# The last matrix product of a decode step in two column groups of 256 columns instead of four of 128

## The chip, the core and the metric

The kernel runs on one core of a Trainium2 chip. The metric is the device time of one execution in microseconds, the median of several runs. The core has four engines that matter here: TensorE (PE; its weight loads are listed as PEld), VectorE (DVE), ScalarE (ACT) and GpSimd (POOL). SyncE (SP) issues the transfers. TensorE writes to PSUM, and VectorE and ScalarE copy from PSUM into SBUF.

## What is computed

One decode step of a transformer block for 8 sequences, one token each, model width 512: attention over the last 2048 positions of a cache (32 query heads, 8 key/value heads), then an MLP with 1792 hidden units. Each sits behind a LayerNorm and is added to its input. The token shift in the middle of the second block moves everything out of a sequence of length one, so that its product with `w2` is zero.

```python
def _A_ref(x, k_cache, v_cache, wq, wo):
    q = heads(x @ wq)
    k, v = last 2048 positions, each kv head for 4 query heads
    p = _softmax(q k^T * Dh ** -0.5)
    return (p @ v) @ wo

def _B_ref(x, w1, w2, w3, w4):
    ...                                   # hs is zero for S == 1
    x1 = x + hs
    h2 = _gelu(_layernorm(x1, axis=-1) @ w3) @ w4
    return x1 + h2

x = A_x
h = x + _A_ref(_layernorm(x, axis=-1), A_k_cache, A_v_cache, A_wq, A_wo)
h2 = h + _B_ref(_layernorm(h, axis=-1), B_w1, B_w2, B_w3, B_w4)
return h2
```

The change concerns the last line: `... @ w4`, the addition of `x1` and `h`, and the way of the sum into the output.

## The kernel before

The order of the work on each engine is written out by hand: the program appends operations to one list for each engine, each with the semaphores that it waits for, and emits the lists at the end. [...]

The bulk of the time is the stream of keys and values (16 tiles each of 2 MB), transposed and multiplied as they land. All big loads are issued by SP in a fixed order: keys, values, the parts of `wo`, then `w3` (L672) and, last of all, `w4` in three parts (L676). The parts cover rows 0 to 7, 8 to 11 and 12 to 13 of 14 blocks of 128 hidden units (`W4_AT = (0, 8, 12, FC)`, L634).

The tail after the last value tile goes: output projection (L490, L511, L520), LayerNorm statistics (L569 to L601), the product with `w3` (L588, 56 products of eight columns), Gelu (L613), and the last product with `w4`. The names that matter for the last product:

- `gT` holds the Gelu's result, hidden unit by row, 8 sequences and 24 zeros as 32 columns for each of the 14 blocks. It is the stationary operand, so a product has 32 output rows.
- `z_ps` is a part of one PSUM bank (`S_ps[1]`). Output column block `nb` (128 of the 512 columns) is put into rows 32 `nb` to 32 `nb` + 31, columns 0 to 127: the four blocks use the four column groups of TensorE (`tile_position=(0, 32 * nb)`).
- `pe_w4` (L640) runs over the blocks of one part of `w4`, and for each over the four column blocks, with `w4_sb` as the moving operand of 128 columns. It is called three times, and each call waits for its own part of `w4`; the first also for both halves of `gT` and for the bank.
- `pe_fin` (L630) adds the residual: `fin`, in a high and a low bf16 part (`fr[:, 0]` and `fr[:, 1]`, written at L621 and L622), is multiplied with the identity into the same accumulation. Its eight products stand between the first and the second part of `w4`.
- L647 to L652: four copies of 8 rows by 128 columns from `z_ps` to `out_sb`, alternately by VectorE and ScalarE, each waiting for the last product.
- L693: SP stores `out_sb` when the last copy of either engine is done. Nothing else is left then.

Of the kernel before, what the change touches and what calls it, by code (L numbers as in the profile page):

```python
# [7 lines left out]
ACT = mybir.ActivationFunctionType  # L8
# [3 lines left out]
B = 8  # L12
D = 512
H = 32
DH = 128
# [7 lines left out]
FC = F // 128  # L23
FG = FC // 2
KC = D // 128
# [49 lines left out]
def bass_sequential_preLN__sliding_block_cached__mixer_s_mlp__decode_kernel(  # L75
# [23 lines left out]
    with es:  # L99
# [7 lines left out]
        ident_b = sb([128, 128], dt.bfloat16, "ident_b")  # L107
# [10 lines left out]
        w4_sb = sb([128, FC, D], dt.bfloat16, "w4_sb")  # L118
# [53 lines left out]
        fr = qflat[:, 0:2 * KC * 32].rearrange("p (a n x) -> p a n x", a=2, n=KC)  # L172
        gT = qflat[:, 2 * KC * 32:(2 * KC + FC) * 32].rearrange("p (f x) -> p f x", f=FC)
        out_sb = orow[0:B, 0, :]
# [4 lines left out]
        S_ps = [ps_t([128, 512], dt.float32, f"S_ps{i}") for i in range(2)]  # L179
# [13 lines left out]
        PE, AC, DV, PO, SP = (Engine(S(n)) for n in ("s_pe", "s_act", "s_dve", "s_pool", "s_sp"))  # L193
# [21 lines left out]
        e = DV.op(lambda e: e.bn_stats(st6[:, :], x_sb[:, :]), X)  # L215
        e = DV.op(lambda e: e.bn_aggr(mv[:, :], st6[:, :]), e)
        e = PO.op(lambda e: e.tensor_scalar(rstd[:, :], mv[:, 1:2], EPS, None, ALU.add), e)
        e = PO.op(lambda e: e.tensor_tensor(rstd[:, :], rstd[:, :], half[0:B, 0:1], ALU.pow), e)
# [8 lines left out]
        e = DV.op(lambda e: e.tensor_reduce(hsq[:, :], ident_f[:, :].rearrange("p (u h) -> p h u", u=4), AX.X, ALU.add))  # L227
# [31 lines left out]
        e = PE.op(pe_xT, e_xln, e_idb)  # L259
# [6 lines left out]
        for j in range(2):  # L266
# [9 lines left out]
            if j == 0:  # L276
                e = AC.op(lambda e: e.activation(qrow[:, 0, :], S_ps[0][:, :], ACT.Copy, scale=inv_sqrt_dh), e_q)  # L277
            else:
                e = DV.op(lambda e: e.tensor_scalar(qrow[:, 1, :], S_ps[1][:, :], inv_sqrt_dh, None, ALU.mult), e_q)  # L279
# [285 lines left out]
        def bc(a):  # L565
            return bass.AP(tensor=a.tensor, offset=a.offset, ap=[a.ap[0], [0, KC], [1, B]])


        e = DV.op(lambda e: e.tensor_reduce(hsum[:, :], vr(hT_ps[:, 0:NH]), AX.X, ALU.add), e_wo[-1])  # L569
# [30 lines left out]
        e = AC.op(lambda e: e.activation(s2[:, :], vsum[:, :], ACT.Sqrt, bias=eps2[:, :], scale=1.0), e_vs)  # L600
        e_r2 = DV.op(lambda e: e.reciprocal(r2[:, :], s2[:, :]), e)  # L601

        def bcf(t):
            a = t[:, :]
            return bass.AP(tensor=a.tensor, offset=a.offset, ap=[a.ap[0], [0, FH], [1, B]])
# [3 lines left out]
        for n in range(2):  # L609
            cs = slice(n * FH * B, (n + 1) * FH * B)  # L610
            e = DV.op(lambda e, n=n, cs=cs: e.tensor_tensor(v3(g_x[:, cs]), v3(y_ps[n][:, 0:FH * B]), bcf(r2),
                                                            ALU.mult), e_y[n], e_r2)
# [3 lines left out]
        e = PO.op(lambda e: e.tensor_scalar(r1[:, :], vsum[:, :], EPS * (1.0 + EPS), None, ALU.add), e_vs)  # L616
        e = PO.op(lambda e: e.tensor_tensor(r1[:, :], r1[:, :], half[:, :], ALU.pow), e)
        e = DV.op(lambda e: e.tensor_tensor(v3(xb[:, :]), v3(hc[:, :]), bc(r1[:, :]), ALU.mult), e)
# [2 lines left out]
        e_fr = DV.op(lambda e: e.tensor_copy(fr[:, 0, :, 0:B], v3(fin[:, :])), e_fin, e_gz)  # L621
        e_fr = DV.op(lambda e: e.tensor_tensor(fr[:, 1, :, 0:B], v3(fin[:, :]), fr[:, 0, :, 0:B], ALU.subtract), e_fr)  # L622

        z_ps = S_ps[1][:, 0:DH]

        def pe_fin():
            def f(e):
                for part in range(2):
                    for nb in range(KC):
                        ins = e.matmul(z_ps[32 * nb:32 * (nb + 1), :], fr[:, part, nb, :], ident_b[:, :],  # L630
                                       start=False, stop=False, tile_position=(0, 32 * nb), skip_group_check=True)
                return ins
            PE.op(f, e_fr)
        W4_AT = (0, 8, 12, FC)  # L634
        for n, waits in enumerate(((*e_gT, free[1]), (), ())):
            lo, hi = W4_AT[n:n + 2]
            def pe_w4(e, lo=lo, hi=hi):
                for fc in range(lo, hi):
                    for nb in range(KC):
                        ins = e.matmul(z_ps[32 * nb:32 * (nb + 1), :], gT[:, fc, :],  # L640
                                       w4_sb[:, fc, nb * 128:(nb + 1) * 128], start=(fc == 0), stop=(fc == FC - 1),
                                       tile_position=(0, 32 * nb), skip_group_check=True)
                return ins
            if n == 1:
                pe_fin()
            e_z = PE.op(pe_w4, (sem_w4[n], 16), *waits)
        for nb in range(KC):  # L647
            to, got = out_sb[:, nb * 128:(nb + 1) * 128], z_ps[32 * nb:32 * nb + B, :]
            if nb % 2:
                e_outa = AC.op(lambda e, to=to, got=got: e.activation(to, got, ACT.Copy), e_z)  # L650
            else:
                e_outd = DV.op(lambda e, to=to, got=got: e.tensor_copy(to, got), e_z)  # L652

        def load_k(j):
            dma(SP, knat[:, j % NK, :],
# [72 lines left out]
```

## Time and profile before

| | us |
|---|---|
| runs, median (lowest to highest of 3) | 194.07 (194.07 to 194.26) |
| the profiled execution | 193.93 |
| its span | 192.6 |
| PE busy in the span | 153.9 |
| DVE busy | 99.6 |
| ACT busy | 95.2 |
| last w4 product's end to the copies' start (L640 to L652) | 190.50 to 190.56 |
| the store's issue (L691) | 191.25 to 191.63 |

The span is the part of an execution between the first and the last recorded instruction; 1.3 us lie around it. For most of it the transfers are the limit: the 16 DMA engines move some 430 GB/s in nearly each slice, and in the last two slices of 40 they fall to 363 and 73. In the groups of the profile, `128*32 128x128` after a product means a stationary operand of 128 rows by 32 columns and a moving one of 128 by 128; `x56` is the number of instructions. The granted clock is a share of TensorE's full clock.

### The profile page before, as it was taken

What the parts mean: (1) busy time and instruction counts of PE and PEld (TensorE: products, weight loads), DVE (VectorE), ACT (ScalarE), POOL (GpSimd) and SP (SyncE); (2) the same over time, 40 slices, a digit from 0 to 9 for tenths busy, and PEclk for the clock granted to TensorE, in tenths of its full rate; (3) what the DMA queues carried; (4) which work ended last, traced back from release to release, by engine and by line L of the source; (5) the groups of instructions that cost most, each with busy time, mean ns of one, the idle gap of its engine ahead of it and who ended that gap; (6) DMA issues with size and microseconds to landing.
All of it is one profiled execution on the core that took longest, in us unless ns stands there. A gap on an engine that the chain in (4) does not pass through costs nothing.

```text
span 192.6 us, 4536 instructions
## 1 busy us (share of the span) xinstructions
PE 153.9 (80%) x2034; PEld 103.4 (54%) x2034; DVE 99.6 (52%) x206; ACT 95.2 (49%) x139; POOL 8.4 (4%) x17
## 2 busy tenths in 40 slices
PE   0002989998999889988999896979999999998654
PEld 0001667774667466645665564646765674445453
DVE  7710364755375537553755273725572747372432
ACT  3000567784358435853585355735673585232251
POOL 8300000000000000000000000000000000000130
PEclk9999999999999999999999999999999999999975
DMA  5999999999999999999999999999999999999991
GB/s 219 436 436 425 432 429 432 429 432 429 425 429 417 429 429 434 432 436 429 425 432 429 432 422 436 425 422 432 432 432 432 429 429 417 437 412 425 411 363 73
DMA packets 6851, 79.47 MB, mean 413 GB/s; under 512 B 672, under 2 KB 688, under 8 KB 2096
## 3 DMA queue, kind: packets, MB, share of 16 engines
q1 hardware_dynamic: 6816, 79.18, 96.9%
q8 instruction: 16, 0.26, 0.5%
q14 instruction: 3, 0.02, 0.0%
q10 hardware_dynamic: 16, 0.01, 0.0%
HBM read 79.18 MB, written 0.01 MB: 411 GB/s over the span
## 4 chain that ended last, share of the span: by engine, by line
DMA 68%; PE 26%; DVE 3%; SPq 2%; issue 1%
DMA knat<-in_A_k_cache_dram 32%; DMA w_sb<-in_B_w_dram 16%; PE kT_ps L323 12%; DMA vnat<-in_A_v_cache_dram 11%; DMA wbig<-in_A_wq_dram 9%; PE S_ps L343 4%; PE S_ps L445 2%; PE o_rows L445 2%; PE S_ps L271 2%; SPq L197 2%; PE S_ps L640 1%; PE sm L462 1%; DVE mcol L362 1%; DVE kT_sb L333 1%; DVE qblk L293 1%
## 5 line engine op out<-in xcount | busy, mean ns | idle before, releaser
L331 ACT ACTIVATE kT_sb<-kT_ps 128x1024 bf16<-128x1024 bf16 x64 | 65.5, 1025 | 34.8 <-PE kT_ps L323 34.5
L323 PE MATMUL kT_ps<-turn_b,knat 128*128 128x128 bf16 x1024 | 68.1, 220 | 9.6 <-DMA knat<-in_A_k_cache_dram 9.6
L323 PEld LDWEIGHTS kT_ps<-turn_b,knat 128*128 128x128 bf16 x1024 | 57.4, 98 | 25.0 <-DMA knat<-in_A_k_cache_dram 13.4
L333 DVE COPY kT_sb<-kT_ps 128x1024 bf16<-128x1024 bf16 x64 | 44.4, 693 | 33.4 <-PE kT_ps L323 32.6
L343 PE MATMUL S_ps<-kT_sb,qblk 128*32 128x512 bf16 x256 | 26.9, 390 | 0.7 <-DVE qblk L293 0.7
L445 PE MATMUL o_rows<-vnat,pT_sb 128*64 128x512 bf16 x128 | 15.3, 382 | 0.6 <-issue 0.6
L452 DVE TENSOR_TENSOR orow<-o_rows,orow 128x512 bf16<-128x512 f32 x8 | 5.5, 692 | 18.1 <-ACT orow L451 18.1
L445 PE MATMUL S_ps<-vnat,pT_sb 128*64 128x512 bf16 x112 | 13.4, 382 | 0.2 <-DMA vnat<-in_A_v_cache_dram 0.2
L452 DVE TENSOR_TENSOR qrow<-S_ps,qrow 128x512 bf16<-128x512 f32 x8 | 5.5, 692 | 15.0 <-ACT qrow L451 15.0
L451 ACT ACTIVATE orow<-o_rows 128x512 bf16<-128x512 f32 x8 | 4.8, 597 | 15.5 <-PE o_rows L445 15.5
L343 PEld LDWEIGHTS S_ps<-kT_sb,qblk 128*32 128x32 bf16 x256 | 7.2, 93 | 9.2 <-issue 5.0
L271 PE MATMUL S_ps<-wbig,xlnT 128*32 128x512 bf16 x32 | 3.6, 629 | 10.1 <-DMA wbig<-in_A_wq_dram 10.1
L451 ACT ACTIVATE qrow<-S_ps 128x512 bf16<-128x512 f32 x8 | 4.8, 597 | 12.6 <-PE S_ps L445 12.6
L445 PEld LDWEIGHTS o_rows<-vnat,pT_sb 128*64 128x64 bf16 x128 | 6.7, 110 | 7.0 <-issue 2.2
L421 DVE TENSOR_TENSOR pT_sb<-o_rows,own_f 128x512 bf16<-128x512 f32 x14 | 9.5, 682 | 0.5 <-PE o_rows L408 0.5
L277 ACT ACTIVATE qrow<-S_ps 128x512 bf16<-128x512 f32 x1 | 0.6, 597 | 17.2 <-PE S_ps L271 17.2
L445 PEld LDWEIGHTS S_ps<-vnat,pT_sb 128*64 128x64 bf16 x112 | 5.8, 110 | 6.0 <-issue 1.1
L418 ACT ACTIVATE pT_sb<-S_ps,own_f 128x128 bf16<-128x128 f32 x28 | 7.9, 373 | 1.2 <-PE S_ps L408 1.2
L607 POOL MEMSET qrow<- 128x704 bf16 x1 | 0.7, 684 | 172.0 <-PE sm L462 172.0
L380 ACT ACTIVATE P_sb<-S_ps,negcol 128x512 bf16<-128x512 f32 x8 | 5.5, 687 | 4.3 <-DVE negcol L379 4.3
L271 PEld LDWEIGHTS S_ps<-wbig,xlnT 128*32 128x32 bf16 x32 | 1.2, 138 | 11.6 <-issue 11.6
L279 DVE TENSOR_SCALAR qrow<-S_ps 128x512 bf16<-128x512 f32 x1 | 0.7, 692 | 11.5 <-PE S_ps L271 11.5
(110 smaller groups left out, 137.4 us busy)
## 6 DMA issues: line engine op xcount, KB each, us to landing
knat<-in_A_k_cache_dram SPq DMA_DIRECT2D x16, 2048.0 KB, 20.1
vnat<-in_A_v_cache_dram SPq DMA_DIRECT2D x15, 2048.0 KB, 20.0
wbig<-in_A_wq_dram SPq DMA_DIRECT2D x1, 4096.0 KB, 16.5
wbig<-in_A_wo_dram SPq DMA_DIRECT2D x4, 1024.0 KB, 22.2
knat<-in_A_v_cache_dram SPq DMA_DIRECT2D x1, 2048.0 KB, 19.4
w_sb<-in_B_w_dram SPq DMA_DIRECT2D x1, 1792.0 KB, 29.0
w_sb<-in_B_w_dram SPq DMA_DIRECT2D x1, 1024.0 KB, 31.1
w_sb<-in_B_w_dram SPq DMA_DIRECT2D x1, 512.0 KB, 23.6
```

The costliest lines, as they stand in the source:

```text
L197: e.dma_start(dst, src).then_inc(sem, 16)
L271: ins = e.matmul(S_ps[j][32 * u:32 * (u + 1), :], xlnT[:, kc, :], wq_v[:, kc, n:n + R * DH], start=(kc == 0), stop=(kc == KC - 1), tile_po ...
L323: ins = e.matmul(kT_ps[i % 2][:, n * 128:(n + 1) * 128], knat[:, j % NK, c * DH:(c + 1) * DH], turn_b[:, :], is_transpose=True)
L331: e_lo[i] = AC.op(lambda e: e.activation(kT_sb[:, i % NKT, 0:W // 2], kT_ps[i % 2][:, 0:W // 2], ACT.Copy), e_Tlo[i], e_QK.get(i - NKT))
L333: e_hi[i] = DV.op(lambda e: e.tensor_copy(kT_sb[:, i % NKT, W // 2:W], kT_ps[i % 2][:, W // 2:W]), e_Thi[i], e_QK.get(i - NKT))
L343: ins = e.matmul(S_ps[b % 2][32 * t:32 * (t + 1), :], qblk[:, b, KQ * q + t, at:at + H], kT_sb[:, i % NKT, :].rearrange("p (n t a) -> p t ...
L380: e_exp[b] = AC.op(lambda e: e.activation(P_sb[:, b % NPB, :], S_ps[j][:, :], ACT.Exp, bias=negcol[:, b:b + 1], scale=1.0, accum_out=lcol[ ...
L418: e = AC.op(lambda e, t=t: e.activation(to[:, :, t, :], got[:, :, t, :], ACT.Copy, scale=own_f[:, t:t + 1]), *waits)
L421: e = DV.op(lambda e: e.tensor_tensor(to, got, own, ALU.mult), *waits)
L445: ins = e.matmul(bank[64 * u:64 * (u + 1), :], pT_sb[:, b % 2, n, :].rearrange("p (x q) -> p q x", q=NQ)[:, q, :], v_tile(m)[:, n * 512:(n ...
L451: e_ohi[m] = AC.op(lambda e: e.activation(to[:, 0, :], bank[:, :], ACT.Copy), e_PV[m], e_O.get(m - 2))
L452: e_olo[m] = DV.op(lambda e: e.tensor_tensor(to[:, 1, :], bank[:, :], to[:, 0, :], ALU.subtract), e_ohi[m])
```

## The change

The 512 output columns are split into two blocks of 256 in place of four of 128. Block `u` goes to rows 64 `u` to 64 `u` + 31 of the bank, columns 0 to 255. Each of the 14 blocks of hidden units takes two products with 256 moving columns in place of four with 128. The eight products of `pe_fin` still have 128 columns each; two of them now share a column group, side by side in its columns. VectorE copies one block of 8 x 256 and ScalarE the other.

```diff
-        z_ps = S_ps[1][:, 0:DH]
+        z_ps = S_ps[1][:, 0:D // 2]
...
                 for part in range(2):
                     for nb in range(KC):
-                        ins = e.matmul(z_ps[32 * nb:32 * (nb + 1), :], fr[:, part, nb, :], ident_b[:, :],
-                                       start=False, stop=False, tile_position=(0, 32 * nb), skip_group_check=True)
+                        u, h = divmod(nb, 2)
+                        ins = e.matmul(z_ps[64 * u:64 * u + 32, h * 128:(h + 1) * 128], fr[:, part, nb, :],
+                                       ident_b[:, :], start=False, stop=False,
+                                       tile_position=(0, 64 * u), skip_group_check=True)
...
                 for fc in range(lo, hi):
-                    for nb in range(KC):
-                        ins = e.matmul(z_ps[32 * nb:32 * (nb + 1), :], gT[:, fc, :],
-                                       w4_sb[:, fc, nb * 128:(nb + 1) * 128], start=(fc == 0), stop=(fc == FC - 1),
-                                       tile_position=(0, 32 * nb), skip_group_check=True)
+                    for u in range(2):
+                        ins = e.matmul(z_ps[64 * u:64 * u + 32, :], gT[:, fc, :],
+                                       w4_sb[:, fc, u * (D // 2):(u + 1) * (D // 2)],
+                                       start=(fc == 0), stop=(fc == FC - 1),
+                                       tile_position=(0, 64 * u), skip_group_check=True)
...
-        for nb in range(KC):
-            to, got = out_sb[:, nb * 128:(nb + 1) * 128], z_ps[32 * nb:32 * nb + B, :]
-            if nb % 2:
-                e_outa = AC.op(lambda e, to=to, got=got: e.activation(to, got, ACT.Copy), e_z)
-            else:
-                e_outd = DV.op(lambda e, to=to, got=got: e.tensor_copy(to, got), e_z)
+        e_outd = DV.op(lambda e: e.tensor_copy(out_sb[:, 0:D // 2], z_ps[0:B, :]), e_z)
+        e_outa = AC.op(lambda e: e.activation(out_sb[:, D // 2:D], z_ps[64:64 + B, :], ACT.Copy), e_z)
```

## The prediction

> **What bounds the kernel now.** I read the chain of waits first, then the timeline of the last stretch, then the granted clock there, then the groups of instructions for prices. The chain, cut to the stretch from 165 us on (start, us, what):
>
> ```profile
> 157.09 31.09 DMA w_sb<-in_B_w_dram
> 188.19 0.04 issue
> 188.23 1.04 PE S_ps L640 x31
> 189.27 0.21 PE S_ps L630 x8
> 189.49 0.60 PE S_ps L640 x16
> 190.09 0.02 issue
> 190.11 0.43 PE S_ps L640 x7
> ...
> 190.56 0.28 DVE orow L652
> 190.84 0.03 issue
> 190.88 0.28 DVE orow L652
> ```
>
> The load of w4 holds the kernel until 188.19 us. From there to the second copy's end at 191.16 the end is set by the very code that is changed: nothing else runs beside it that could hide a longer stage. The timeline shows that TensorE still waits twice in there for the rest of w4 (the bracket is the idle time before, and what ended it):
>
> ```profile
> 189.47 0.35 PEld L640 LDWEIGHTS S_ps<-w_sb,qrow 128*32 128x32 bf16 x16 [0.26 <-DMA w_sb<-in_B_w_dram]
> 189.47 1.04 PE L640 MATMUL S_ps<-w_sb,qrow 128*32 128x128 bf16 x24
> 190.10 0.14 PEld L640 LDWEIGHTS S_ps<-w_sb,qrow 128*32 128x32 bf16 x8 [0.28 <-DMA w_sb<-in_B_w_dram]
> ```
>
> So the second part of w4 (rows 8 to 11 of 14) is there at 189.47 and the third (12, 13) at 190.10. The windows give the clock (columns: length, busy time of PE, PEld, DVE, ACT, POOL, granted clock, DMA share, GB/s):
>
> ```profile
> 185.20:185.40 0.20, 0.00 (x0) 0.00 (x0) 0.06 (x1) 0.10 (x1) 0.05 (x1) 1.00 1.02 379
> 185.40:185.60 0.20, 0.00 (x0) 0.00 (x0) 0.00 (x0) 0.20 (x1) 0.20 (x1) 0.51 1.05 399
> 188.00:190.60 2.60, 2.26 (x64) 1.47 (x64) 0.35 (x3) 0.04 (x1) 0.00 (x0) 0.50 0.30 114
> ```
>
> The whole last product runs at half the clock, which fell at 185.4 us after a stretch of products of eight columns each.
>
> **The pace of the products, now.** Narrow stretches of the timeline show that the four products of one row block start together:
>
> ```profile
> 190.19 0.32 PE L640 MATMUL S_ps<-w_sb,qrow 128*32 128x128 bf16 x4
> ```
>
> One of them lasts 0.313 us (median of L640), and all four lie within 0.32. Such groups start at 188.63, 188.74, 188.84, 188.95 and 189.06: one each 0.107 us. That is the time of 128 columns at this clock, and the four column groups share it. The query product early in the kernel has the same form with 512 columns; its weight loads, four at a time, come every 0.43 us, four times 0.107:
>
> ```profile
> 18.44 0.18 PEld L271 LDWEIGHTS S_ps<-wbig,xlnT 128*32 128x32 bf16 x4 [0.25 <-issue]
> 18.87 0.18 PEld L271 LDWEIGHTS S_ps<-wbig,xlnT 128*32 128x32 bf16 x4 [0.25 <-issue]
> ```
>
> So a column group takes one column per 0.83 ns at half clock, whatever the other groups do. (The clock row says 1.00 there, but 0.632 us for a product of this form against 0.390 at L343, and the spacing, are those of half clock; I go by them.)
>
> **The change, part by part.** *The w4 products.* 56 products of 128 columns in four column groups become 28 of 256 columns in two. No row shows two groups of 256 columns at half clock. The nearest is L445, two groups, 512 columns, full clock: 16 products in 1.87 us on the chain, so with 0.38 for the last one (1.87 - 0.38) / 7 = 0.213 us a pair, the time of 512 columns in one group. Half the columns at half the clock give 0.213 again. The bounds: 0.107 a pair, if the pace were not set by columns, and 0.427, if the two did not overlap. I take 0.213, because L445 is the nearest row and L271 gives the same by columns. A row block thus costs twice the 0.107 of today: two of four column groups stand empty. Half as many weight loads (28 for 56, 0.146 us each) brings nothing: they already lie beside the products, 12 of them in each 0.2 us.
>
> *The eight products of L630* keep their 128 columns, but their order is now group 0, 0, 2, 2, and again. Two in a row on one group follow one another: L462, whose eight go to one group at full clock, takes 0.44 us on the chain, 0.055 each. [...] Today these eight take 0.21. They wait for the DVE result of L622, done at 188.34; TensorE comes to them 1.6 us later, so that cover is ample.
>
> *The copies.* Two per engine one behind the other become one per engine with 256 columns. DVE: 0.282 us for 128 columns here, 0.692 for 512 from PSUM (L497), so 1.07 ns a column and 0.42 for 256. ScalarE: 0.270 and 0.597 (L496), so 0.38, which ends first. Bounds: 0.28 and 0.69 for DVE. Today it takes 190.56 to 191.16, 0.60. Saved: 0.18. Nothing is queued behind either copy but the store's wait on SP, which moves with them. No load is moved; all SP issues before the store stay where they are.
>
> *The sum, as a clock.* Start 188.23, as now. Eight pairs: 8 x 0.213 = 1.70, to 189.93 (now 189.06). L630: 0.43, to 190.36. Its second part of w4 has been there since 189.47, so that wait is gone; the third is reached at 190.36 + 4 x 0.213 = 191.21 and has been there since 190.10, so that one is gone too. The sixth pair starts at 190.36 + 5 x 0.213 = 191.43, its second product 0.107 later, 191.53 (the last start now: 190.19). It lasts 0.313 + 0.107 = 0.42, to 191.95; 0.06 to the copies as now (190.50 to 190.56): 192.01. Copy 0.42: 192.43 against 191.16. **The end moves by 1.27 us**: 1.34 for the later last start, 0.11 for its length, less 0.18 for the copies. In other terms: 14 x 0.107 + 0.32 = 1.82 us of added product time, of which some 0.48 go into the two waits. The profiled execution, 193.93 us with a span of 192.6, would become 195.20. It lies 0.14 below the median shown, 194.07; from the median I get 195.34 and say 195.3.
>
> **Rivals.** *The clock comes back inside the longer stage.* In the query stage dense products began at 18.06 us, and the products from 21.60 on run at 32 in 1.96 us, 0.061 each, full pace: about 3.5 us at half clock. From 188.23 the same 3.5 us end at 191.7, after the last start of 191.53: too late to help. Against that, the stage has few products just ahead (L588, until 187.3), which could count. If the clock returned at 190.8, the 0.73 us to the last start would halve, and the last product would last 0.27 (at full clock 0.379 less 0.107): 0.52 less, 194.8. If at 190.0, 0.77 + 0.15 less: 194.4.
> [...]
>
> *Not slower: full clock from early on in the stage.* At full clock a pair costs 0.107: the eight are through at 189.09, L630 at 189.30, both waits for w4 stay (189.47, 190.11), the last start is 190.22, it lasts 0.27, the copies start at 190.55 and end at 190.97: 0.19 under today, 193.9 from the median. To end under today the clock would have to return by about 189.3 (the saving of half the rest has to reach 1.27). For it: only that the change makes the stage denser. Against: it fell 2.8 us before the stage, in a stretch that is not changed, and does not rise in it now.
>
> *Not slower either: the pace is set by the instruction, 0.107 / 4 = 0.027 us each.* Then 28 are cheaper than 56, the waits for w4 stay, the last start remains 190.19, the last lasts 0.42, and the end is 191.09: 0.07 less, 194.0. It decides when a pair costs under about 0.145 us, since the end moves by 13 times the pair's cost. Against it: four starts within 0.01 us, then none for 0.1; and L271 at four times the columns takes four times the time.
> [...]
>
> *The two groups do not overlap.* 28 x 0.213 + 0.85 = 6.81 us: the last start at 194.83, 198.6 in all; with the clock back after 3.5 us half of the last 3.1 is saved, 197.1. Against it: L445's pairs.
>
> **How the numbers follow.** The forecast 0.70; the clock back late, still slower, 0.13; the clock back early 0.06; pace by instructions 0.05; no overlap 0.06. What a measurement of this kernel can tell from no change is 0.2%, 0.39 us (the runs spread by 0.19): slower is above 194.46. The forecast, the late clock and no overlap are slower: 0.89. Of the other two 0.09 lie within 0.2%, 0.02 faster. The likeliest case by itself: down to 195.1 (no lag, 0.11, and spread), up to 195.65 (L630 at 0.85 without lag, 0.32 more). To hold eight in ten the range goes down over most of the late clock, to 194.5, and up by the spread of the runs, to 195.8.
>
> **What would show it.** In the profile after: L640 as 28 products of 128x256, some 0.42 us each, two starting every 0.213; its rows 8 and 12 no longer waiting for w_sb; L630 over some 0.43; granted clock 0.50 from 185.4 to beyond 191.9; one copy of 0.42 and one of 0.38, starting near 192.0; the span near 193.9. I am wrong if pairs come closer than 0.2 us, if the clock rises before 191.5, or if TensorE still waits for the third part of w4.

## The result

The change makes the kernel slower: 195.25 us in the median of 6 runs (194.99 to 195.96) against 194.07 (193.99 to 194.26), a ratio of 1.0068 with a 95% interval of 1.0054 to 1.0081. The forecast was 195.3 in a range of 194.5 to 195.8. The profiled execution took 195.35 us with a span of 194.0.

### The profile page after: what moved, and what is told of

Its sections match the earlier page's. It is cut to its first block, busy times and chain, and to the rows that moved or that the text cites. A ratio compares the mean times of both kernels' runs of the same rounds, so it can differ in the third digit from the quotient of the medians.

```text
span 194.0 us, 4470 instructions
## 1 busy us (share of the span) xinstructions
PE 154.4 (80%) x1998; PEld 104.4 (54%) x2006; DVE 99.2 (51%) x205; ACT 95.1 (49%) x138; POOL 8.4 (4%) x17
## 4 chain that ended last, share of the span: by engine, by line
DMA 67%; PE 26%; DVE 3%; SPq 2%; issue 1%
DMA knat<-in_A_k_cache_dram 32%; DMA w_sb<-in_B_w_dram 16%; PE kT_ps L323 12%; DMA vnat<-in_A_v_cache_dram 11%; DMA wbig<-in_A_wq_dram 9%; PE S_ps L343 4%; PE S_ps L445 2%; PE o_rows L445 2%; PE S_ps L271 2%; SPq L197 2%; PE S_ps L642 2%; PE sm L462 1%; DVE mcol L362 1%; DVE kT_sb L333 1%; DVE qblk L293 1%
## 5 line engine op out<-in xcount | busy, mean ns | idle before, releaser
L445 PE MATMUL o_rows<-vnat,pT_sb 128*64 128x512 bf16 x128 | 15.3, 382 | 0.6 <-issue 0.6
L445 PE MATMUL S_ps<-vnat,pT_sb 128*64 128x512 bf16 x112 | 13.4, 382 | 0.2 <-DMA vnat<-in_A_v_cache_dram 0.2
L445 PEld LDWEIGHTS o_rows<-vnat,pT_sb 128*64 128x64 bf16 x128 | 6.8, 110 | 7.0 <-issue 2.2
L445 PEld LDWEIGHTS S_ps<-vnat,pT_sb 128*64 128x64 bf16 x112 | 5.8, 110 | 6.0 <-issue 1.1
```

What stands on the lines that cost most here:

```text
L445: ins = e.matmul(bank[64 * u:64 * (u + 1), :], pT_sb[:, b % 2, n, :].rearrange("p (x q) -> p q x", q=NQ)[:, q, :], v_tile(m)[:, n * 512:(n ...
```

## The profile after

The timeline of the kernel after, from the first w4 product on (start, length, engine, line, operation):

```profile
188.45 1.89 PE L642 MATMUL S_ps<-w_sb,qrow 128*32 128x256 bf16 x16 [0.89 <-DMA w_sb<-in_B_w_dram]
...
190.13 0.64 PE L631 MATMUL S_ps<-ident_b,qrow 128*32 128x128 bf16 x8
...
190.56 1.50 PE L642 MATMUL S_ps<-w_sb,qrow 128*32 128x256 bf16 x12
192.09 0.38 ACT L651 ACTIVATE orow<-S_ps 8x256 bf16<-8x256 f32 x1 [3.99 <-PE S_ps L642]
192.09 0.41 DVE L650 CAST orow<-S_ps 8x256 bf16<-8x256 f32 x1 [3.51 <-PE S_ps L642]
```

The first pair still waits for w4, and then nothing does: the two waits in the middle of the stage have no successor here, and the 12 products after the residual's follow in one piece. From the first w4 product to the copies it is now 192.09 - 188.45 = 3.64 us; before it was 190.56 - 188.23 = 2.33. I call this the stretch below. It is the better measure for small things, because the start itself moves: here the first part of w4 landed at 188.41, before at 188.19. That is not the change's doing: the chain below has this load begin at 157.38, before at 157.09, long ahead of the first changed line.

The chain of waits of the kernel after names TensorE for all of the stretch:

```profile
157.38 31.03 DMA w_sb<-in_B_w_dram
...
188.45 1.89 PE S_ps L642 x16
190.35 0.43 PE S_ps L631 x8
190.77 1.30 PE S_ps L642 x12
192.07 0.02 issue
192.09 0.41 DVE orow L650
```

The windows of the kernel after (length, busy time of PE, PEld, DVE, ACT, POOL, granted clock, DMA share, GB/s) show when the clock fell and when it came back:

```profile
185.20:185.40 0.20, 0.12 (x2) 0.01 (x1) 0.04 (x1) 0.00 (x0) 0.00 (x0) 0.70 1.01 376
185.40:185.60 0.20, 0.00 (x0) 0.00 (x0) 0.15 (x1) 0.01 (x1) 0.00 (x0) 0.50 1.03 379
188.40:192.00 3.60, 3.55 (x36) 2.44 (x36) 0.19 (x1) 0.00 (x0) 0.00 (x0) 0.50 0.19 72
192.00:192.20 0.20, 0.05 (x2) 0.00 (x0) 0.11 (x1) 0.11 (x1) 0.00 (x0) 0.73 0.00 0
192.20:192.40 0.20, 0.00 (x0) 0.00 (x0) 0.20 (x1) 0.20 (x1) 0.00 (x0) 1.00 0.00 0
```

It is 0.50 for the whole stage and 1.00 when the copies already run. A mean of 0.73 from 192.00 to 192.20 puts the rise at about 192.1; in the same way 0.70 puts the fall at 185.3.

## The experiments

The theory, an estimate from the rows of the kernel before, is that a column group takes a fixed time per column (0.83 ns at half clock), that the clock sets this time, and that two groups of 256 columns therefore cost twice as much per row block as four of 128. The rivals are a pace set by the number of products, groups that do not overlap, and effects of the copies. Diffs are against the kernel after where nothing else is said.

### The number of products

```diff
-                    for u in range(2):
-                        ins = e.matmul(z_ps[64 * u:64 * u + 32, :], gT[:, fc, :],
-                                       w4_sb[:, fc, u * (D // 2):(u + 1) * (D // 2)],
+                    for h in range(2):
+                        for u in range(2):
+                            n = 2 * u + h
+                            ins = e.matmul(z_ps[64 * u:64 * u + 32, h * 128:(h + 1) * 128], gT[:, fc, :],
+                                           w4_sb[:, fc, n * 128:(n + 1) * 128],
...
```

> The two column groups of the change, but with 56 products of 128 columns again (group 0, group 2, group 0, group 2 for each row block), and the rest as in the change. If the price is the columns that one group has to take at half clock (my theory), each row block still costs 0.213 us, the stretch from the first w4 product to the start of the copies stays at the 3.64 us of the change (before: 2.33), and the time is about 195.2. If the pace is set by the number of products, 0.027 us each, the stretch goes to about 2.3 and, with the shorter copies kept, the time to about 193.9.

Measured: 195.14 us (195.00 to 195.69), ratio 1.0058 [1.0046, 1.0070]. The timeline of this kernel:

```profile
188.88 1.89 PE L644 MATMUL S_ps<-w_sb,qrow 128*32 128x128 bf16 x32 [0.93 <-ACT qrow L613]
190.54 0.66 PE L631 MATMUL S_ps<-ident_b,qrow 128*32 128x128 bf16 x8
190.97 1.51 PE L644 MATMUL S_ps<-w_sb,qrow 128*32 128x128 bf16 x24
192.52 0.41 DVE L652 CAST orow<-S_ps 8x256 bf16<-8x256 f32 x1 [2.83 <-PE S_ps L644]
```

With the 56 products of before in the two groups of after, the stretch is 192.52 - 188.88 = 3.64, to the last digit that of the change. Whether 28 or 56 products did the work was without effect here, at a granted clock of 0.50 in both, and the columns that one group had to take were the price.

### All columns in one group

```diff
+                    ins = e.matmul(z_ps[0:32, :], gT[:, fc, :], w4_sb[:, fc, :],
+                                   start=(fc == 0), stop=(fc == FC - 1),
+                                   tile_position=(0, 0), skip_group_check=True)
...
+        e_outd = DV.op(lambda e: e.tensor_copy(out_sb[:, :], z_ps[0:B, :]), e_z)
```

> All 512 columns in one column group: 14 products of 128x512, eight of the residual one behind the other, one VectorE copy of 8x512. By columns at half clock a row block costs 0.427 us, 5.97 for 14, and the residual's eight 0.85: the last product would start 6.4 us after the first. If the clock comes back some 3.5 us into the dense stage, the rest goes at double pace: copies near 5.4 us after the first product, of 0.69, and 197.3 in all. If it stays at half: copies at about 6.85, and 198.8. If the number of products set the pace, it would be 194.5 or less.

Measured: 197.15 us (197.01 to 197.80), ratio 1.0164 [1.0151, 1.0177]. Its timeline and its clock:

```profile
188.41 3.59 PE L640 MATMUL S_ps<-w_sb,qrow 128*32 128x512 bf16 x8 [0.90 <-DMA w_sb<-in_B_w_dram]
191.80 0.68 PE L630 MATMUL S_ps<-ident_b,qrow 128*32 128x128 bf16 x8
192.31 1.46 PE L640 MATMUL S_ps<-w_sb,qrow 128*32 128x512 bf16 x6
193.81 0.68 DVE L647 CAST orow<-S_ps 8x512 bf16<-8x512 f32 x1 [5.28 <-PE S_ps L640]
```

```profile
188.40:191.60 3.20, 3.19 (x8) 1.18 (x9) 0.13 (x1) 0.00 (x0) 0.00 (x0) 0.50 0.19 72
192.00:193.80 1.80, 1.77 (x15) 0.80 (x12) 0.00 (x0) 0.00 (x0) 0.00 (x0) 1.00 0.00 0
```

The stretch is 5.40 us, as worked out for a clock that returns some 3.5 us into the dense stage. From 191.60 to 192.00 the mean clock was 0.60, which puts its return at 191.9, 3.5 us after the first w4 product. The first eight row blocks take 191.80 - 188.41 = 3.39, 0.42 each, at half clock; the last six, behind the residual's, ran at a granted clock of 1.00 and took 1.46 in all. With 0.38 for the last one, as at L445 in the kernel before, that is (1.46 - 0.38) / 5 = 0.22 each. This shows both halves of the theory in one run: 14 products cost more than 56 (a stretch of 5.40 against 3.64), and the price per column halved when the clock was back.

### The residual's order

```diff
-                    for nb in range(KC):
+                    for nb in (0, 2, 1, 3):
                         u, h = divmod(nb, 2)
```

> The change with the residual's eight products taken in alternation of the two groups (0, 2, 0, 2, ...). By the working of the prediction the order 0, 0, 2, 2 makes the second group lag by 0.107 us until the end; alternation would take that off: the stretch from the first w4 product to the copies 3.53 us, the time 195.15. The trace of the change shows both groups starting each pair together, without a lag; by that the stretch stays at 3.64 and the time at 195.25.

Measured: 195.17 us (194.94 to 196.01), ratio 1.0060 [1.0046, 1.0074]. The first w4 product started at 189.21 and the copies at 192.85, a stretch of 3.64 as with the order 0, 0, 2, 2. The lag of the prediction does not show. The timeline of the change itself shows this too: of the residual's products, in the order 0, 0, 2, 2, two start together, and so does the pair of w4 products behind them:

```profile
190.13 0.32 PE L631 MATMUL S_ps<-ident_b,qrow 128*32 128x128 bf16 x2
...
190.56 0.43 PE L642 MATMUL S_ps<-w_sb,qrow 128*32 128x256 bf16 x2
```

The next run shows how far ahead of its place in the program a product started.

### One group's products ahead of the other's

```diff
-                for fc in range(lo, hi):
-                    for u in range(2):
+                for u in range(2):
+                    for fc in range(lo, hi):
```

> The change with the loops of each part of w4 turned: first all products of column group 0, then all of group 2 (8 and 8, 4 and 4, 2 and 2). If products start strictly in program order, nearly nothing overlaps: about 0.43 us for each row block, some 5.5 us from the first w4 product to the copies with the clock back on the way, 197.1. If each column group takes its products from the queue by itself, as the eight products of the residual let one think, the stretch stays at 3.64 and the time at 195.2.

Measured: 196.04 us (195.44 to 196.40), ratio 1.0101 [1.0085, 1.0117]: between the two times that were forecast. Lines of its timeline: narrow stretches shortly after the start and 0.9 us later, the products up to the residual's first, and the copy:

```profile
188.53 0.61 PE L642 MATMUL S_ps<-w_sb,qrow 128*32 128x256 bf16 x2 [0.93 <-DMA w_sb<-in_B_w_dram]
...
189.14 0.63 PE L642 MATMUL S_ps<-w_sb,qrow 128*32 128x256 bf16 x3
...
188.53 2.08 PE L642 MATMUL S_ps<-w_sb,qrow 128*32 128x256 bf16 x13 [0.93 <-DMA w_sb<-in_B_w_dram]
190.21 0.42 PE L631 MATMUL S_ps<-ident_b,qrow 128*32 128x128 bf16 x2
...
192.99 0.41 DVE L650 CAST orow<-S_ps 8x256 bf16<-8x256 f32 x1 [3.94 <-PE S_ps L642]
```

A product lasts 0.42 and one of the same group follows after 0.213, so two of one group were in flight at a time. Until 189.35 there are two; at 189.40 there are three. The second group's first product, ninth in the program, thus begins at about 189.35, when the fifth does (188.53 + 4 x 0.213 = 189.38), not when the first does, and not behind the eighth. The residual's first product shows the same a second time: it is the 17th in the program and starts at 190.21, when 13 have started. The stretch is 4.46, which is 3.64 plus this 0.82. So TensorE did start a product ahead of earlier ones that waited for another column group, but here only some four places ahead. The residual's order 0, 0, 2, 2 lies within that reach, and the change's own alternation needs none of it. What limits the reach was not tried.

### The copies

The copies of the change undone, two of 8x128 on each engine:

```diff
+        for h in range(2):
+            c = slice(h * 128, (h + 1) * 128)
...
+            e_outd = DV.op(lambda e, c=c: e.tensor_copy(out_sb[:, c], z_ps[0:B, c]), e_z)
+            e_outa = AC.op(lambda e, c=c, c2=c2: e.activation(out_sb[:, c2], z_ps[64:64 + B, c], ACT.Copy), e_z)
```

> The change with its copies undone: two of 8x128 on each engine, one behind the other. Theory: the copies take 0.60 us as before in place of 0.41, the stretch of products stays at 3.64, and the time is 0.18 above the change, some 195.4. Rival: the second copy of each engine hides behind something (the store's issue); then the time is that of the change, 195.25.

Measured: 195.28 us (195.17 to 195.50), ratio 1.0062 [1.0049, 1.0075]. The stretch is 3.64 once more, but the two copies take less than expected:

```profile
192.01 0.43 ACT L654 ACTIVATE orow<-S_ps 8x128 bf16<-8x128 f32 x2 [3.99 <-PE S_ps L642]
192.01 0.48 DVE L653 CAST orow<-S_ps 8x128 bf16<-8x128 f32 x2 [3.07 <-PE S_ps L642]
```

On VectorE it is 0.48 in place of 0.60: the second copy starts 0.21 after the first, before that has ended, where in the kernel before it started 0.32 after. The difference could lie in the blocks' order or in the PSUM rows. The kernel before with its copies dealt out by halves tells the two apart (diff against the kernel before):

```diff
-            if nb % 2:
+            if nb >= 2:
                 e_outa = AC.op(...)
```

> The kernel before with its four copies dealt out otherwise: VectorE the first two column blocks, ScalarE the last two. In the run with four copies two on one engine took 0.48 us, with starts 0.21 apart, against 0.59 and 0.32 in the kernel before. If that lies in the order of the blocks on an engine, the copies here take 0.48 and the time is 193.95; if it lies in both reading from one PSUM row range, they take 0.59 and the time is 194.07.

Measured: 194.13 us (193.79 to 194.24), ratio 0.9999 [0.9990, 1.0007]. Its copies:

```profile
190.52 0.59 DVE L652 CAST orow<-S_ps 8x128 bf16<-8x128 f32 x2 [1.87 <-PE S_ps L640]
190.52 0.56 ACT L650 ACTIVATE orow<-S_ps 8x128 bf16<-8x128 f32 x2 [2.71 <-PE S_ps L640]
```

So it is not the blocks' order. Two copies overlapped by 0.06 us on VectorE and 0.09 on ScalarE where they read the same eight PSUM rows, and had a gap of 0.02 to 0.03 where the second read other rows. The two kernels also differ in the columns: with four copies the second reads other columns than the first, here it reads the same columns of other rows. That the same columns alone keep two operations apart is ruled out by a pair of VectorE operations in the kernel before, both on the same rows and columns of PSUM, of which the second started at 183.49, before the first had ended at 183.57:

```profile
183.38 0.19 DVE L569 TENSOR_REDUCE hsum<-S_ps 128x8 f32<-128x32 f32 x1 [0.45 <-PE S_ps L520]
183.49 0.18 DVE L570 COPY hs<-S_ps 128x32 f32<-128x32 f32 x1
```

For VectorE that leaves the rows, as far as these three pairs go; for ScalarE it stays open whether the rows or the columns decide. The saving of the change, 0.59 to 0.41, then has two parts: about 0.11 comes from reading one row range in place of two, 0.07 from one instruction in place of two.

### The clock

The change, and the kernel before, with extra products of 128x512 into an unused PSUM bank in TensorE's idle stretches of the tail. They stand behind each of the last two `pe_O`, ahead of `pe_hr`, of the mean, of the variance and of the w3 product, between its halves and behind it. There are 22 of them, not the 18 that the expectations say. They add nothing to the output.

```diff
+        def keep(count, *waits):
+            def f(e):
+                for n in range(count):
+                    ins = e.matmul(kbank[1], ident_b[:, :], PT_sb[:, :], start=True, stop=True)
+                return ins
+            PE.op(f, *waits)
...
+            if b == LAST:
+                keep(4 - q, e_pT[LAST, 1])
...
+        keep(3)
         pe_hr()
+        keep(1)
...
+        keep(3)
...
+        keep(3)
+        e_y = [pe_w3(0, FH, e_u, (sem_w3, 16))]
+        keep(1)
+        e_y.append(pe_w3(FH, FC))
+        keep(4)
```

> The change, with 18 extra products of 128x512 into an unused PSUM bank put into TensorE's idle stretches between the last value product and the first w4 product (their results are used by nothing). If the price is columns at half clock, and these products keep the clock at 1.00 through the w4 product, then a pair costs 0.107 us, TensorE waits for the second and third part of w4 again, the stretch from the first w4 product to the copies is 2.3 us (with the change: 3.64), and the time 193.9. If the clock is not what makes the pairs cost 0.213, the stretch stays at 3.64 and the time at 195.2 or above.

> The kernel before with the same 18 extra products. At full clock a row block costs 0.053 us, which only lengthens the two waits for w4: stretch 2.2 us in place of 2.33, time about 193.95. With the waits setting the end in both, the price of the two column groups is then gone: this kernel and the change with the same products differ by the copies (0.41 against 0.60) less 0.11 for the longer last pair, the change being ahead by some 0.1 us. If two groups cost something at full clock too, beyond what the waits hide, this one is ahead.

Measured: 193.87 us (193.64 to 194.05) for the change with them, ratio 0.9989 [0.9980, 0.9998]; 193.95 (193.81 to 194.13) for the kernel before with them, ratio 0.9994 [0.9985, 1.0003]. The window over the w4 products and then the chain of the change with the extra products:

```profile
188.60:190.40 1.80, 1.80 (x35) 1.45 (x36) 0.21 (x2) 0.00 (x0) 0.00 (x0) 1.00 0.32 118
```

```profile
188.71 0.98 PE S_ps L658 x16
189.69 0.22 PE S_ps L647 x8
189.91 0.79 PE S_ps L658 x12
190.71 0.02 issue
190.73 0.41 DVE orow L666
```

The clock is 1.00 and the same 28 products in two groups need half the time: eight pairs and the residual's eight in 1.20 in place of 2.32 on the two chains. The loss of the change, 1.18 us, is gone. The chain of the kernel before with the extra products shows why four groups gain nothing there:

```profile
176.85 13.25 DMA w_sb<-in_B_w_dram
190.10 0.04 issue
190.14 0.32 PE S_ps L656 x8
```

It still waits for the third part of w4. The extra products behind w3 are in the way of the change, though: they end at 188.71, and it comes to the third part of w4 only at 190.29. So the last pair of runs has two of them in place of four at that point (`keep(2)`).

> The change with extra products again, but two in place of four behind the w3 product. In the run with four they ended at 188.71 and held up the first w4 product, which could have started at about 188.4, and TensorE came to the third part of w4 only at 190.3. With two, the first pair starts at 188.4, the third part is waited for until 190.1, the copies start at 190.55 in place of 190.73, and the time is 193.7, if the clock stays at 1.00. If it falls with so few, the time is 194.5 or more.

> The kernel before with the same extra products, two in place of four behind the w3 product. It waited for the third part of w4 until 190.14 already with four, so an earlier start of w4 brings nothing: copies at 190.49, time 193.95. Against the change with the same extra products it is then behind by the copies' 0.18 less 0.06, some 0.15 us.

Measured: 193.74 us (193.64 to 193.92), ratio 0.9989 [0.9980, 0.9997], and 193.79 us (193.65 to 194.02), ratio 0.9989 [0.9980, 0.9998]. The granted clock was 1.00 from 176 us to the end of the copies in both. The chain of the change with two:

```profile
188.39 1.05 PE S_ps L658 x16
189.44 0.22 PE S_ps L647 x8
189.66 0.44 PE S_ps L658 x8
190.10 0.04 issue
190.14 0.41 PE S_ps L658 x4
190.56 0.02 issue
190.58 0.41 DVE orow L666
```

Its first w4 product starts at 188.39 and its copies at 190.58, as expected. Of its kind this is the fastest, some 0.2 us under the kernel before, but that is 0.11%, with an interval that nearly touches 1. The kernel before did better than expected with two (193.79 for 193.95), and the medians of the two differ by 0.05, less than their spread: with the clock up, four groups or two make no difference that these runs can tell. In both, the landing of the last 256 KB of w4 set the end: the weight loads of the third part waited for it until 190.14 and 190.03 us, and the copies started 0.44 and 0.35 later.

## Why the prediction was right

- *A pair costs 0.213 us.* Pairs started at 188.64, 188.85, 189.07, 189.28 and so on; L642 lasts 0.421 (0.42 forecast). The row that gave it, two groups of 512 columns at full clock, and the rule by columns were both sound: the runs with 56 products in two groups and with one group bear out the second (stretches of 3.64 and 5.40), and the runs with the extra products the effect of the clock (1.20 for 2.32 us).
- *The two waits for w4 vanish.* So they did, and swallowed part of the added product time.
- *The residual's eight take 0.43* (190.13 to 190.56). So they did; ahead of this trace no run showed it, and it was an estimate. *The second group then lags by 0.107.* No run shows this term of the sum: in its place both groups start together at 190.56, and with the residual's eight in alternation the stretch is the same 3.64. Nor does any show the 0.85 of the range and of the last rival, which is eight times 0.107, with the eight one behind the other. In the change two products started together at 190.13, though two of one group come first in the program, and in the run with one group's products ahead of the other's a product started some four places early.
- *The copies: 0.60 to 0.42, 0.18 saved.* 0.41 measured, ScalarE 0.38 as forecast. The row for 512 columns was an addition (L497, 0.692); the plain copy of 512 columns in the run with one group takes 0.68, so that it was a fair stand-in. That the price of two copies went with the rows that they read (0.48 us from one row range, 0.59 from two) was not foreseen; the forecast took it from the very copies that it replaced, and so was not hurt by it.
- *The sum.* From the first w4 product to the copy's end it was 191.16 - 188.23 = 2.93 and became 192.50 - 188.45 = 4.05: 1.12 more, where 1.27 was forecast. The lag that did not come is 0.107 of the 0.15 between them. The medians differ by 1.18. That 195.25 is so near to 195.3 is in part luck: in two of the six runs (195.94 and 195.96) the mean clock (0.956 and 0.955) was as low as in the traces in which it fell five microseconds sooner (0.956 and 0.955), which the forecast does not contain. The other four have a median of 195.16, which is 1.09 above the kernel before.
- *The clock stays at 0.50 beyond the last product.* It rose at about 192.1, within 0.1 us of the last product's end. The rival by which it returns inside the stage lost narrowly in this execution. In the four other traces with two groups and no extra products the clock fell earlier, at about 180.5 twice, at 183.0 and at 183.6, and was 0.50 to the end of the stage as well, so that no trace with two groups shows an early return. The kernel with one group is the one that a return inside the stage shortened: at 191.9, to 5.40 us where 6.85 was worked out for half clock throughout.
- *The rivals.* Pace by instructions and no overlap are out by the runs on the number of products and on one group. Full clock from early on comes out close to its working in the runs whose extra products kept the clock at 1.00: with two extra products behind w3 the copies start at 190.58 (190.55 forecast) and the time is 193.74 (193.9). The 193.87 with four agrees better by chance, since there the extra products hold up the start of w4. The change by itself did not keep the clock up (0.50 for the whole stage).

## What to carry to other kernels

Where a product with 32 output rows takes one of four column groups, as here, count what one group has to stream: that set the time, not the number of products (3.64 us with 28 and with 56). Giving up half of the column groups to save copies doubled the time of a row block, from 0.107 to 0.213 us, and can pay only where that time is hidden; even there these runs could not tell a gain (193.74 against 193.79). In a tail behind a stretch of tiny products, look at the granted clock first: the same change cost 1.18 us at a clock of 0.50 and nothing that could be told at 1.00. Before counting on a clock trick, find what sets the end next; here it was the last piece of the weights, and there were some 0.2 us to be had.

## What the runs showed of the hardware

- Products left their program order: with runs of products for one column group, the other group's first started about four places ahead of its turn (0.82 us after the start in place of 1.7).
- Consecutive copies from PSUM overlapped where they read the same rows (two of 8x128 on VectorE in 0.48 us), and did not where the second read other rows (0.59); ScalarE 0.43 and 0.56, though there the columns, which differ too, were not ruled out.
- The clock's fall lay elsewhere from one profiled execution to the next. In the kernel after it came at 185.3, and in the profiled executions of the runs on the number of products and on the residual's order already at about 180.5. In the first of these two the output projection ran at half pace too (16 products in 1.93 us, in the run with one group 1.04), and the first w4 product waited for ScalarE until 188.88. It took 195.69 where the others of that kernel took 195.00 to 195.19, and the two longest of the kernel after, 195.94 and 195.96, had the lowest mean clock (0.956 and 0.955, the others 0.974 to 0.982). The kernel before spreads less (193.83 to 194.42 over all its runs), though its two longest runs, 194.35 and 194.42, also have its lowest mean clock, 0.958. That its waits for w4 take up the rest is likely, but not shown.
- When the clock came back differed as well. In the kernel after it rose at 192.1 and in the run with one group at 191.9, in both 6.8 us after its fall (185.3 and 185.1). In the run with 56 products, with the fall at 180.5, it did not return by the stage's end, though dense products ran from 188.88 to 192.5; in the run with one group's products ahead of the other's it fell at 183.6, and TensorE was busy without a break from 188.8 to 192.8 and the clock still 0.50. What sets the moments of the fall and of the return was not shown.
